# The first product of a gated mixing kernel: seven block products with shared sums, four of them split a second time, accumulated onto blocks in PSUM

## The chip, the cores and the metric

The kernel runs on one core of one Trainium2 chip. The metric is the device time of one execution in microseconds (us); lower is better. The core has TensorE (PE in the profile, with PEld for its weight loads), VectorE (DVE), ScalarE (ACT), GpSimd (POOL) and SyncE (SP), which issues most of the transfers (DMA). Operands lie in SBUF; a matmul adds its result into PSUM, which is as large as eight blocks of 128 x 512 float32, and DVE or ACT reads it from there.

## What is computed

```
a = x @ Cd.T ; b = x @ Sd.T          # x: 2048 x 1024, Cd, Sd: 1024 x 1024 (cosines, sines)
y = Cs @ a - Ss @ b                  # Cs, Ss: 2048 x 2048
h = relu(x @ w1 + b1) ** 2           # w1: 1024 x 3584
o = h @ w2 + b2                      # w2: 3584 x 1024
g = sigmoid((x * gate_w).sum(-1))
out = g * y + (1 - g) * o            # 2048 x 1024, all float32
```

The change touches the first line above all: x times the 1024 x 2048 matrix W that holds Cd and Sd side by side.

## The kernel before, in words

**Precision.** Every float32 operand is split in two halves of a faster matmul type: ScalarE copies it into `hi` (line 176), VectorE forms `lo` = operand - hi (line 194), and three matmuls (hi hi, hi lo, lo hi; line 261) take the place of one. Each operand that PE uses so costs one ACT copy and one DVE subtraction of 128 x 1024 elements.

**Blocks, steps and groups.** All data moves in blocks of 128 x 2 x 512 float32, of 512 KB. A *step* is the product of one stationary block with one moving block: 4 rows x 2 halves x 3 matmuls = 24 matmuls of 128 x 128 x 512. A `Group` is the set of steps that add up in the same two PSUM tiles (two banks each). When a group has run its `k` steps, its `done` function takes the two PSUM tiles up, the first after half of the last step (when two of the four rows are through), the second at its end. A tile taken up for the first time goes to SBUF as an ACT copy (line 285), later ones as a DVE addition or subtraction (line 287). A group may have several `done` functions: the PSUM tiles are then not cleared, and the next product adds to what they hold.

**Seven products for eight.** Each of the four matrix products is cut in 2 x 2 parts, and seven products of sums of parts replace eight products (tables `LEFT`, `RIGHT`, `INTO`; `INTO` says to which parts of the result a product is added). In `a1` (lines 304 to 360) the order is 2, 7, 4, 5, 6, 1, 3. Each of these products is itself 2 x 2 x 2 blocks: eight steps in four groups of two steps. Products 7 and 6 (`TWICE`) are cut a second time, and take seven steps in groups of one. That makes 5 x 8 + 2 x 7 = 54 steps in `a1`; the whole kernel has 362.

**Sums.** An `Operand` with two parts loads both and adds them on DVE (line 175); where the operation is an addition and the product is not the first, the second part is added by a GpSimd-issued accumulating DMA instead (line 157). For the products cut twice, class `Sum` makes the first-level sums (line 234) and `Operand` the second-level ones (line 175, `sum<-part`).

**Where blocks live.** SBUF has 55 slots (line 18); `take` and `give` (lines 85 to 93) hand them out first in, first out. The results `a` are stored to DRAM and loaded again in `a2`; the results `b` stay in SBUF. PSUM is a pool of four tiles of two banks, used in turn (lines 71 and 253): one group holds two.

**The order of the work.** Lines 537 to 608 write the program out, step by step. Before step i, blocks for steps up to i + 12 are loaded as far as slots are free; operands of step i + 3 are summed and copied to `hi` at the latest, `lo` of step i + 2 at the latest; earlier (up to nine steps) only while slots and the planner's own clock for DVE allow (lines 585 to 600). Then the step's matmuls and take-ups are written. The framework orders each engine's queue once more by when its model expects an instruction to be ready; the trace shows the order that came out. After `a1` follow `a2` (lines 400 to 441), and twice `h_stage` and `o_stage`.

Of the kernel before, what the change touches and what calls it, by code (L numbers as in the profile page):

```python
# [19 lines left out]
TWICE = (7, 6)  # L20
# [16 lines left out]


LEFT_A = {**LEFT, 1: ((0, 0), (1, 1), SUB), 6: ((1, 0), (0, 0), ADD), 7: ((0, 1), (1, 1), ADD)}
RIGHT_A = RIGHT  # L40
INTO_A = {1: ((0, 0, 1), (1, 1, -1)), 2: ((1, 0, 1), (1, 1, -1)), 3: ((0, 1, 1), (1, 1, -1)),
          4: ((0, 0, -1), (1, 0, 1)), 5: ((0, 0, -1), (0, 1, 1)), 6: ((1, 1, 1),), 7: ((0, 0, 1),)}
# [13 lines left out]
def gated_mix_kernel(ctx: ExitStack, tc: tile.TileContext, x4, xn, w4, ct, w1a, w1b, w2, b1, b2, gw, out):  # L56
# [14 lines left out]
    psum = ctx.enter_context(tc.tile_pool(name="psum", bufs=4, space=bass.MemoryType.PSUM))  # L71
    dram = ctx.enter_context(tc.tile_pool(name="dram", bufs=1, space=bass.MemoryType.DRAM))

    free = deque(ctx.enter_context(tc.tile_pool(name=f"slot{i}", bufs=1)) for i in range(SLOTS))
    home = {}
# [24 lines left out]
    class Near:  # L100


        def __init__(self, name):
            self.name, self.slot, self.uses, self.done = name, None, 0, False
# [20 lines left out]
    class Operand:  # L125


        def __init__(self, blocks, width=512, dma=False):
            self.width = width
            self.op = blocks[2] if len(blocks) == 3 else None  # L130
            self.blocks = list(blocks[:2]) if self.op else list(blocks[:1])
            self.added = None
            if dma and self.op == ADD:
                self.op, self.added = None, self.blocks.pop()
            self.uses = 0
            self.cuts = [(slice(0, 2), slice(0, width))]
            for b in self.blocks:
                if isinstance(b, Near):
                    b.uses += 1
# [14 lines left out]
        def load(self, engines):  # L154
            run(self.load_parts(engines))
            if self.added is not None:
                nc.gpsimd.dma_start(self.slots[0], self.added, accum_op=ADD)

        def extra(self):

            return max(2 + (self.op is not None) - self.room(), 0)

        def vector_time(self):
            return VEC[0] + VEC[1] * self.width / 512

        def sum_parts(self):
# [4 lines left out]
            self.src = src[0] if not self.op else mine[0] if mine else take("sum")  # L171
            self.hi = take("hi", F32R)
            for k, c in self.cuts:
                if self.op:
                    nc.vector.tensor_tensor(self.src[:, k, c], src[0][:, k, c], src[1][:, k, c], op=self.op)  # L175
                nc.scalar.activation(self.hi[:, k, c], self.src[:, k, c], AF.Copy)  # L176
                yield
            if self.op:
                give(*mine[1:])
                self.let_go()  # L180

        def sum(self):
            run(self.sum_parts())
            return self.vector_time() if self.op else 0.0

        def let_go(self):
            for b in self.blocks:
                if isinstance(b, Near):
                    b.used()

        def rest_parts(self):
            self.lo = take("lo", F32R)
            for k, c in self.cuts:
                nc.vector.tensor_tensor(self.lo[:, k, c], self.src[:, k, c], self.hi[:, k, c].bitcast(F32),  # L194
                                        op=SUB)
                yield
            if not self.op:
                self.let_go()
            if self.op or not isinstance(self.blocks[0], Near):
                give(self.src)  # L200

        def rest(self):
            run(self.rest_parts())
            return self.vector_time()
# [6 lines left out]
    class Sum(Near):  # L211


        def __init__(self, blocks):
            super().__init__("part")
            self.op = blocks[2] if len(blocks) == 3 else None
            self.blocks = list(blocks[:2]) if self.op else list(blocks[:1])

        def extra(self):
            return 0  # L220

        def room(self):
            return len(self.blocks)

        def load(self, engines):
            self.raws = [take("part") for b in self.blocks]
            for b, t in zip(self.blocks, self.raws):
                next(engines).dma_start(t, b)

        def sum(self):  # L230
            self.slot, self.done = self.raws[0], True
            if not self.op:
                return 0.0
            nc.vector.tensor_tensor(flat(self.slot), flat(self.slot), flat(self.raws[1]), op=self.op)
            give(self.raws[1])
            return VEC[0] + VEC[1]

        def rest(self):
            return 0.0

    class Group:


        def __init__(self, rows, k, *done):

            self.rows, self.k, self.done, self.at = rows, k, done, 0
# [3 lines left out]

        def run(self, st, mv, by_part=False):
            if self.at == 0:
                self.ps = [psum.tile([P, 2, 512], F32, name="ps") for _ in range(self.rows // 2)]
# [5 lines left out]
            for r, kk, n in mms:  # L259
                a, b = ((st.hi, mv.hi), (st.hi, mv.lo), (st.lo, mv.hi))[n]  # L260
                nc.tensor.matmul(self.ps[r // 2][:, r % 2, :], a[:, kk, r * P:(r + 1) * P],  # L261
                                 b[:, kk, :], start=self.at == 1 and kk + n == 0,
                                 stop=ends and kk == 1 and n == 2, skip_group_check=self.at > self.k)
                if ends and r % 2 and kk == 1 and n == 2:
                    self.done[self.at // self.k - 1][0](r // 2, self.ps[r // 2])

# [36 lines left out]

    def a1():
        order = (2, 7, 4, 5, 6, 1, 3)
        first, last = touches(order, INTO_A)
        def take_up(i, n, q, c, ps, sign, fresh, ends):
            near = ab[n, q, c]
            add_to(near.new() if fresh else near.slot, ps, -sign if n else sign, fresh)
            if ends:  # L310
                near.done = True
                if n == 0:
                    stores.append((a_far[q, c], near))

        def twice(p):

            order2 = (4, 3, 7, 1, 5, 6, 2)
            first2, last2 = touches(order2, CHAINED)
            part_a = {(m, q): Sum(blocks_of(LEFT_A[p], lambda i, j, m=m, q=q: x4[2 * i + m, j, q]))
                      for m in range(2) for q in range(2)}  # L320
            part_b = {(q, c): Sum(blocks_of(RIGHT_A[p], lambda j, n, c=c, q=q: w4[n, c, j, q]))
                      for c in range(2) for q in range(2)}
            groups = {}
            for p2 in order2:
                def done(p2):
                    def f(rp, ps):
                        for m, c, sign2 in CHAINED[p2]:
                            for i, n, sign in INTO_A[p]:
                                take_up(i, n, 4 * i + 2 * m + rp, c, ps, sign * sign2,
                                        first[i, n] == p and first2[m, c] == p2,  # L330
                                        last[i, n] == p and last2[m, c] == p2)
                    return f, 2 * sum(first[i, n] == p and first2[m, c] == p2
                                      for m, c, _ in CHAINED[p2] for i, n, _ in INTO_A[p])

                on = {4: 7, 1: 6}.get(p2)
                if p2 not in (7, 6):
                    groups[on] = group = Group(4, 1, *(done(e) for e in (p2, on) if e))
                else:
                    group = groups[p2]
                st = Operand(blocks_of(LEFT[p2], lambda m, q: part_a[m, q]))  # L340
                mv = Operand(blocks_of(RIGHT[p2], lambda q, c: part_b[q, c]))
                step(st, mv, group)

        for p in order:
            if p in TWICE:
                twice(p)
                continue
            mvs = [[Operand(blocks_of(RIGHT_A[p], lambda j, n, c=c, q=q: w4[n, c, j, q]), dma=p != order[0]) for q in range(2)]
                   for c in range(2)]
            for m in range(2):  # L350
                sts = [Operand(blocks_of(LEFT_A[p], lambda i, j, m=m, q=q: x4[2 * i + m, j, q]), dma=p != order[0])
                       for q in range(2)]
                for c in (m, 1 - m):
                    def done(rp, ps, p=p, m=m, c=c):
                        for i, n, sign in INTO_A[p]:
# [288 lines left out]
```

## Time and profile before

| what | value |
|---|---|
| median of 3 runs | 1988.97 us (1987.73 to 1989.03) |
| the profiled execution | 1988.42 us, of which the span is 1986.6 us |
| TensorE busy | 1972.6 us, 99% of the span, 8688 matmuls |
| VectorE busy | 1441.5 us, 73% |
| ScalarE busy | 824.2 us, 41% |
| moved by DMA | 421.97 MB, 212 GB/s |
| `a1` in the span | 0 to 306.3 us (1296 matmuls) |

The span is what the profile sees of the program; 1.8 us of the profiled execution lie around it. A row of the profile gives an instruction's own duration. Instructions of one engine overlap: five DVE additions in a row of 1.22 us each take 5.74 us, so one every 1.13 us, and matmuls of 390 ns follow one another every 227 ns.

### The profile page before, as it was taken

To read this page: it belongs to the slowest core of one execution; us is meant where nothing else is said; L and a number is where in the kernel's file an instruction comes from. 1 tells how busy PE (TensorE), PEld (TensorE's weight loads), DVE (VectorE), ACT (ScalarE), POOL (GpSimd) and SP (SyncE) were. 2 spreads that over 40 slices of the span, in tenths; PEclk is the share of its full clock that TensorE was granted. 3 is DMA by queue.
4 is the path that set the end of the run, shared out by engine and by line. 5 is a ranking of instruction groups with operands and counts; after the bars stand their busy time and mean duration, and the time that the engine had idled before them with its cause. 6 is when DMAs were issued, how large, how long until landed. Compare 5 with 4: busy or idle time off the path is not lost.

```text
span 1986.6 us, 22336 instructions
## 1 busy us (share of the span) xinstructions
PE 1972.6 (99%) x8688; PEld 1632.9 (82%) x8688; DVE 1441.5 (73%) x1331; ACT 824.2 (41%) x882; POOL 39.6 (2%) x72
## 2 busy tenths in 40 slices
PE   8999999999999999999999999999999999999999
PEld 6888888888888888888888888888888888888887
DVE  6988989467853579755565867789965667778795
ACT  5613222423432334334654563334456435633342
POOL 0010000000000000000000000000000000000000
PEclk9999999999999999999999999999999999999999
DMA  8673987367654469864454743558854566525671
GB/s 328 202 254 108 334 280 257 133 228 259 233 204 136 159 235 368 332 251 159 146 188 155 274 171 136 169 203 293 322 180 146 171 229 225 191 99 199 216 281 43
DMA packets 126570, 421.97 MB, mean 212 GB/s; under 512 B 13696, under 2 KB 26496, under 8 KB 126464
## 3 DMA queue, kind: packets, MB, share of 16 engines
q1 hardware_dynamic: 117600, 390.92, 55.5%
q0 software_dynamic: 8000, 28.32, 4.2%
q8 instruction: 68, 1.11, 0.2%
q10 hardware_dynamic: 864, 1.31, 0.2%
q14 instruction: 38, 0.31, 0.0%
HBM read 395.33 MB, written 25.17 MB: 212 GB/s over the span
## 4 chain that ended last, share of the span: by engine, by line
PE 99%; DMA 0%; DVE 0%; ACTq 0%; issue 0%; DVEq 0%
PE ps L261 99%; DMA raw<-in_x 0%; ACTq L151 0%; DVE lo L194 0%; DVE o L503 0%; DVEq L640 0%; DVE raw L175 0%; DVEq L194 0%
## 5 line engine op out<-in xcount | busy, mean ns | idle before, releaser
L261 PE MATMUL ps<-hi 128*128 128x512 f32 x2896 | 1127.9, 390 | 6.0 <-ACT hi L176 6.0
L261 PE MATMUL ps<-lo,hi 128*128 128x512 f32 x2896 | 1127.8, 390 | 3.4 <-DVE lo L194 3.4
L261 PE MATMUL ps<-hi,lo 128*128 128x512 f32 x2896 | 1127.7, 390 | 0.0
L176 ACT ACTIVATE hi<-raw 128x1024 fp32r<-128x1024 f32 (+2 forms) x433 | 435.3, 1024 | 797.5 <-PE ps L261 305.0
L261 PEld LDWEIGHTS ps<-hi 128*128 128x128 f32 x2896 | 544.4, 188 | 118.9 <-ACT hi L176 6.0
L261 PEld LDWEIGHTS ps<-lo,hi 128*128 128x128 f32 x2896 | 544.2, 188 | 116.9 <-DVE lo L194 4.2
L261 PEld LDWEIGHTS ps<-hi,lo 128*128 128x128 f32 x2896 | 544.3, 188 | 112.9
L194 DVE TENSOR_TENSOR lo<-raw,hi 128x1024 fp32r<-128x1024 f32 (+2 forms) x433 | 502.2, 1181 | 168.8 <-PE ps L261 69.3
L175 DVE TENSOR_TENSOR raw<-raw 128x1024 f32<-128x1024 f32 (+2 forms) x276 | 322.9, 1177 | 189.8 <-DMA raw<-in_ct 57.9
L287 DVE TENSOR_TENSOR h<-h,ps 128x1024 f32<-128x1024 f32 x84 | 102.3, 1218 | 78.3 <-ACT h L285 45.3
L176 ACT ACTIVATE hi<-sum 128x1024 fp32r<-128x1024 f32 x98 | 103.7, 1060 | 118.3 <-DVE sum L175 99.5
L194 DVE TENSOR_TENSOR lo<-sum,hi 128x1024 fp32r<-128x1024 f32 x98 | 119.6, 1223 | 15.8 <-ACT hi L176 10.2
L463 ACT ACTIVATE h<-h,b1c 128x512 f32<-128x512 f32 x112 | 74.7, 714 | 66.7 <-DVE h L287 66.5
L175 DVE TENSOR_TENSOR sum<-h 128x1024 f32<-128x1024 f32 x70 | 85.4, 1222 | 0.4
L285 ACT ACTIVATE h<-ps 128x1024 f32<-128x1024 f32 x56 | 55.4, 1022 | 48.6 <-PE ps L261 48.6
L465 ACT ACTIVATE h<-h 128x1024 f32<-128x1024 f32 x56 | 58.9, 1052 | 0.8
L503 DVE SCALAR_TENSOR_TENSOR o<-ps,omg,o 128x512 f32<-128x512 f32 x64 | 44.5, 746 | 18.8 <-PE ps L261 18.8
L287 DVE TENSOR_TENSOR a<-a,ps 128x1024 f32<-128x1024 f32 x44 | 52.3, 1217 | 5.2 <-PE ps L261 5.2
L287 DVE TENSOR_TENSOR b<-b,ps 128x1024 f32<-128x1024 f32 x44 | 51.9, 1218 | 0.0
L194 DVE TENSOR_TENSOR lo<-h,hi 128x1024 fp32r<-128x1024 f32 x28 | 34.2, 1221 | 7.5 <-PE ps L261 5.8
L583 POOL DMA_DIRECT2D out<-o x28 | 15.1, 541 | 1014.5 <-DVE o L503 1012.8
L176 ACT ACTIVATE hi<-h 128x1024 fp32r<-128x1024 f32 x28 | 29.3, 1048 | 12.8 <-PE ps L261 12.8
(31 smaller groups left out, 299.9 us busy)
## 6 DMA issues: line engine op xcount, KB each, us to landing
raw<-in_w SPq DMA_DIRECT2D x195, 512.0 KB, 4.5
raw<-in_ct SPq DMA_DIRECT2D x192, 512.0 KB, 5.0
raw<-in_w1a SPq DMA_DIRECT2D x144, 512.0 KB, 4.7
raw<-in_x SPq DMA_DIRECT2D x74, 512.0 KB, 4.7
raw<-a SPq DMA_DIRECT2D x48, 512.0 KB, 4.6
raw<-in_w1b SPq DMA_DIRECT2D x48, 256.0 KB, 3.5
part<-in_w SPq DMA_DIRECT2D x16, 512.0 KB, 9.3
part<-in_x SPq DMA_DIRECT2D x16, 512.0 KB, 8.7
```

The costliest lines, as they stand in the source:

```text
L175: nc.vector.tensor_tensor(self.src[:, k, c], src[0][:, k, c], src[1][:, k, c], op=self.op)
L176: nc.scalar.activation(self.hi[:, k, c], self.src[:, k, c], AF.Copy)
L194: nc.vector.tensor_tensor(self.lo[:, k, c], self.src[:, k, c], self.hi[:, k, c].bitcast(F32), op=SUB)
L261: nc.tensor.matmul(self.ps[r // 2][:, r % 2, :], a[:, kk, r * P:(r + 1) * P], b[:, kk, :], start=self.at == 1 and kk + n == 0, stop=ends a ...
L285: nc.scalar.activation(flat(dst), flat(ps), AF.Copy, scale=float(sign))
L287: nc.vector.tensor_tensor(flat(dst), flat(dst), flat(ps), op=ADD if sign > 0 else SUB)
L463: nc.scalar.activation(dst[:, rr, :], dst[:, rr, :], AF.Relu, bias=b1c[:, f_:f_ + 1])
L465: nc.scalar.activation(flat(dst), flat(dst), AF.Square)
L503: nc.vector.scalar_tensor_tensor(dst[:, rr, :], ps[:, rr, :], (omg if sign > 0 else nomg)[:, t:t + 1], dst[:, rr, :], op0=ALU.mult, op1=AL ...
L583: nc.gpsimd.dma_start(dst, src)
```

## The change

It changes only how `a1` is computed, and what that needs in the helpers.

- *Sums built on one another.* The seven products of `a1` get new factors (`FACTORS`): S1 = A21 + A22, S2 = S1 - A11, S3 = A11 - A21, S4 = A12 - S2, and T1 to T4 alike; they are kept in slots and used again (classes `Sums` and `Part`). Products 1 and 2 take plain parts. No sum is made by an accumulating DMA any more.
- *Four products cut twice.* 1, 5, 3 and 4 run as seven steps each, 2, 6 and 7 as eight: 4 x 7 + 3 x 8 = 52 steps, in the order 1, 2, 5, 3, 6, 7, 4. The second level uses the same tables.
- *Additions in PSUM.* Within a product cut twice, steps 1, 6, 7, 4 share one group (`chain`) and add up in its two tiles; 5 and 3 share another (`other`); 2 has its own (`last`). The order of its steps is 5, 1, 3, 6, 2, 7, 4; for the very first product 1, 5, 3, 6, 2, 7, 4.
- *Products that add to copied blocks.* A group may start `onto` blocks: ACT copies them from SBUF into PSUM (`Group.prepare`, one step ahead), and the matmuls add to them. Products 2, 6 and 7 start onto the eight blocks `part` that hold product 1 (later the sums with it), and step `last` of products 1 and 5.
- *Helpers.* `Operand` is cut in `Part` (load and sum) and `Operand` (`hi` and `lo`); the list of the planner so has up to two entries for an operand of every stage. PSUM tiles come from a list `banks` instead of a rotating pool. Signs in `a2` are moved from the take-up of `b` to `LEFT_C` and `CHAINED_C`; the number of its operations stays.

```diff
-TWICE = (7, 6)
+SUMS_L = {"S1": ((1, 0), (1, 1), ADD), "S2": ("S1", (0, 0), SUB), "S3": ((0, 0), (1, 0), SUB),
+          "S4": ((0, 1), "S2", SUB)}
+SUMS_R = {"T1": ((0, 1), (0, 0), SUB), "T2": ((1, 1), "T1", SUB), "T3": ((1, 1), (0, 1), SUB),
+          "T4": ((1, 0), "T2", SUB)}
+FACTORS = {1: ((0, 0), (0, 0)), 2: ((0, 1), (1, 0)), 3: ("S4", (1, 1)), 4: ((1, 1), "T4"), 5: ("S1", "T1"),
+           6: ("S2", "T2"), 7: ("S3", "T3")}
...
+        def prepare(self):
+            if self.ps is None and len(banks) >= self.rows // 2 and all(b.begun for b in self.onto or ()):
+                pools = [banks.popleft() for _ in range(self.rows // 2)]
+                self.ps = [b.tile([P, 2, 512], F32, name="ps", tag="ps") for b in pools]
+                self.pools = pools
+                for b, t in zip(self.onto or (), self.ps):
+                    nc.scalar.activation(flat(t), flat(b.slot), AF.Copy)
...
-                                 b[:, kk, :], start=self.at == 1 and kk + n == 0,
+                                 b[:, kk, :], start=self.at == 1 and kk + n == 0 and not self.onto,
...
+        def put(dst, ps, ends=False, sign=1):
+            add_to(dst.slot or dst.new(), ps, sign, True)
+            finish(dst, ends)
+
+        def add(dst, ps, ends=False, src=None, sign=1):
+            if src is None:
+                add_to(dst.slot, ps, sign, False)
+            else:
+                nc.vector.tensor_tensor(flat(dst.slot or dst.new()), flat(src.slot), flat(ps), op=ADD)
+                vec(1.22)
+            finish(dst, ends)
...
+        def twice(p, old, new, ends, drop=False):
+            l, r = FACTORS[p]
+            l2 = Sums(lambda m, q: left[m, q].of(l), SUMS_L, True)
+            r2 = Sums(lambda q, c: right[q, c].of(r), SUMS_R, True)
+
+            def takes(first, *where, ends=False):
+                def f(rp, ps):
+                    for m, c in where:
+                        if not first:
+                            add(new[m, c, rp], ps, ends)
+                        elif old:
+                            add(new[m, c, rp], ps, ends, old[m, c, rp])
+                            if drop:
+                                old[m, c, rp].drop()
+                        else:
+                            put(new[m, c, rp], ps, ends)
+                return f, 2 * first * len(where)
+
+            chain = Group(4, 1, takes(True, (0, 0)), takes(False, (0, 1), ends=ends), takes(False, (1, 1), ends=ends),
+                          takes(True, (1, 0), ends=ends))
+            other = Group(4, 1, takes(True, (1, 1)), takes(True, (0, 1)))
+            if old:
+                last = Group(4, 1, takes(False, (0, 0), ends=ends))
+            else:
+                last = Group(4, 1, (lambda rp, ps: put(new[0, 0, rp], ps, ends), 0),
+                             onto=[new[0, 0, rp] for rp in range(2)])
+            begin = ((5, other), (1, chain))
+            for p2, group in (*(begin if steps else begin[::-1]), (3, other), (6, chain), (2, last), (7, chain),
+                              (4, chain)):
+                l_, r_ = FACTORS[p2]
+                step(l2.operand(l_), r2.operand(r_), group)
+
+        def six(k, ps):
+            put(part[k], ps)
+            add(c12[k], ps, True)
+
+        def seven(k, ps):
+            put(part[k], ps)
+            add(c22[k], ps, True)
+
+        twice(1, None, part, False)
+        direct(2, part, 2, lambda k, ps: put(c11[k], ps, True))
+        twice(5, None, c22, False)
+        twice(3, c22, c12, False)
+        direct(6, part, 0, six)
+        direct(7, part, 0, seven)
+        twice(4, part, c21, True, True)
...
+        if 0 <= i < n - 1:
+            steps[i + 1][2].prepare()
```

`direct` runs a product as eight steps in four groups of two, onto the blocks given; `c11` to `c22` are the four parts of the result, of which `c11` and `c21` (the `a`) are stored to DRAM.

More of the change, by code (lines that the diff above doesn't have):

```diff
@@ L302, in gated_mix_kernel @@
     a_far = {(q, c): Kept(f"a{q}{c}") for q in range(8) for c in range(2)}
-    def a1():
[L305 to L309, printed above, removed]
-            if ends:
[L311 to L349, printed above, removed]
@@ L350, in a1 @@
             for m in range(2):
[L351 to L352 removed]
+                sts = [left[m, q].operand(l) for q in range(2)]
                 for c in (m, 1 - m):
[L354 to L358 removed]
+                    group = Group(4, 2, (lambda rp, ps, m=m, c=c: take_up((m, c, rp), ps), slots),
+                                  onto=onto and [onto[m, c, rp] for rp in range(2)])
@@ L401, in a2 @@
         order = (2, 4, 7, 5, 3, 1, 6)
-        first, last = touches(order, CHAINED)
+        first, last = touches(order, CHAINED_C)
         y = {k: Near("y") for k in gy}
@@ L593, in gated_mix_kernel @@
                     break
-                if any(isinstance(b, Near) and not b.done for b in getattr(o, "blocks", ())):
+                if not lo and not ready(o):
                     break
```

220 lines of the change are left out of this document (124 added, 96 removed).

## The prediction, made before the change was run

> **What bounds the kernel now.** First the page's busy shares and its chain of waits, then the chain in order of time, then the waits of PE alone.
>
> ```profile
> PE 1972.6 (99%) x8688; PEld 1632.9 (82%) x8688; DVE 1441.5 (73%) x1331; ACT 824.2 (41%) x882; POOL 39.6 (2%) x72
> ```
> ```profile
> 9.54 1.03 DVE lo L194 x2
> 10.57 0.04 issue
> 10.62 1971.39 PE ps L261 x8686
> 1982.01 0.03 issue
> ```
> ```profile
> PE ps L261 <- ACT hi L176: 6.0, 1, 6.0
> PE ps L261 <- DVE lo L194: 3.4, 1, 3.4
> ```
>
> From 10.62 us on PE runs without a gap; its only two waits lie before. So time is the number of matmuls, the start, and 4.6 us behind the last matmul. Any stall that the change brings is added in full, and no cheaper DVE, ACT or DMA work shortens anything behind the start. The start, by PE's timeline:
>
> ```profile
> 5.96 1.22 PE L261 MATMUL ps<-hi 128*128 128x512 f32 x2 [5.96 <-ACT hi L176]
> 10.62 1.22 PE L261 MATMUL ps<-lo,hi 128*128 128x512 f32 x2 [3.44 <-DVE lo L194]
> ...
> 14.20 1.05 PE L261 MATMUL ps<-hi,lo 128*128 128x512 f32 x2
> 15.05 1.27 PE L261 MATMUL ps<-hi 128*128 128x512 f32 x4
> 16.16 1.08 PE L261 MATMUL ps<-lo,hi 128*128 128x512 f32 x4
> ```
>
> Between 10.62 and 15.05 a matmul starts every 0.43 us, later every 0.23. The windows count 33 matmuls up to 20.0; the other 8655 end at 1982.0, so 0.2267 us each and 5.44 us a step; step k (from 0) ends at 12.52 + 5.44 (k + 1). The slow 10 cost 10 x 0.2 = 2 us.
>
> How tight DVE is, by windows of the products of `a1` (the sixth is the product 6, cut twice) and DVE's timeline in that product:
>
> ```profile
> 137.70:181.20 43.50, 43.50 (x193) 36.03 (x192) 34.14 (x30) 17.36 (x17) 1.06 (x2) 1.00 0.27 97
> 181.20:219.30 38.10, 38.10 (x170) 31.56 (x169) 36.36 (x32) 10.48 (x11) 3.51 (x4) 1.00 0.94 296
> ```
> ```profile
> 213.72 1.22 DVE L175 TENSOR_TENSOR raw<-raw 128x1024 f32<-128x1024 f32 x1
> 214.86 2.35 DVE L287 TENSOR_TENSOR b<-b,ps 128x1024 f32<-128x1024 f32 x2
> ```
>
> Third and fifth figures are the window and DVE: 36.4 of 38.1 us. Product 6 needs 52 DVE operations (8 sums of the first level, 10 of the second, 14 `lo`, 20 take-ups), at one per 1.14 us (five in a row take 5.74) 59 us. DVE managed because it was busy for 34 of 43.5 us in the window before, whose own product 5 has 16 operations (18 us): some 14 were done ahead. Its take-ups came late: step 36 is half through at 211.1, and its first addition starts at 214.86, 3.7 us later. Nobody waited, since between two products in one PSUM group another step always ran.
>
> **The change part by part.**
>
> *Steps.* Of 54 steps in `a1` 52 stay (4 x 7 + 3 x 8): 48 matmuls less, 48 x 0.2267 = 10.9 us off PE, which sets the end. Certain, if PE stays fed.
>
> *Start.* Before, the first step needs two x blocks, their sum and a w block (1.5 MB), and DVE's `lo` waited behind the additions at 7.04 and 8.94. Afterwards it needs one x and one w block and no sum. The w half landed at 5.28, its `hi` took 0.63; so PE could run from about 7 instead of 10.6, 3.6 us earlier at best. The second step then needs three blocks and two sums (T1, S1): at DVE's 13.15 the before had six blocks landed, the after needs five by then; at 0.41 MB per us (the DMA rate after 8 us) that is 1.2 us earlier, about 12; then sum 1.22, `hi` 1.06, `lo` 1.22 makes 15.5, where step 1 began at 17.96. Step 1 and 2 share the group `other`, so step 2 also waits for ACT to read half-way results of step 1: 1.03 us, inside the half step of 2.7 us if ACT's queue is free. The best is -3.6, and +2 if ACT copies of a few later operands go first; I take -2.5, the second step's gain.
>
> *DVE in `a1`.* Before: 52 sums, 68 `lo`, 88 take-ups = 208, as the groups by line count them. Afterwards: first level 8 sums for each of four blocks = 32, second level 8 in each of four products = 32, `lo` 4 x 14 + 3 x 8 = 80, take-ups 4 + 4 + 14 + 14 + 8 + 8 = 52: 196, so 12 x 1.14 = 14 us less in a stage 11 us shorter: 79% against 81%. Off the path in the mean. But by product: 1: 26; 2: 8; 5: 34; 3: 44; 6: 20; 7: 24; 4: 40, where seven steps hold 33 and eight hold 38. So 5, 3 and 4 are over what fits by 1, 11 and 7 operations (1, 12, 8 us) and live on work done ahead in 2, 6 and 7, as product 6 does now.
>
> *Back to back.* New is that steps 7 and 4 of a product cut twice follow each other in the group `chain`: PE may not write a tile before DVE has added it up (1.22 us). The first tile is ready after half a step, so DVE may be 2.72 - 1.22 - 0.1 = 1.4 us late; any more PE waits. No such wait is in the trace. Queued behind it on PE is everything; on DVE ahead of it what belongs to the next three steps. Bounds, from DVE's lateness in the trace: 0 (0.7 us late at 184.65) to 3.7 - 1.4 = 2.3 us each; if DVE does nothing before the planner's latest time, more. In product 4 it then has five operations in most steps, where 4.8 fit, and once six: at the sixth step it is 2.3 us behind, has four operations (4.5 us) ahead of the addition, and ends that 1.25 + 2.3 + 4.5 + 1.15 = 9.2 us after step 5, 3.8 after step 6. The same count gives 3 us in product 3, and 5 in product 5, where 12 operations stand between two take-ups. In products 1 and 5 the step before is taken up by ACT, which leaves DVE free to run ahead. I take 0, 0, 2 and 2 us for products 1, 5, 3 and 4, the lateness that the trace shows: 4 us.
>
> The Trainium skill (TensorE: Matmul & The Clock Gate, section "What's actually happening") speaks against waits of this length: the array runs at half pace until some 3.4 us of work have passed, and again after an idle window as long. The rows of the start agree (3.44 us idle, then 4.4 us slow); a PE that has run at full pace and goes slow again is in no row. By the rule, waits of 2 us cost no more than themselves and the sum stays; one of 3.8 or 5 us would cost 2 us more, 1981 instead of 1979 for one such, and 1991 instead of 1987 in rival A.
>
> *ACT.* `hi` 68 to 80, take-ups 32 to 44, and 28 copies into PSUM: 100 to 152, 54 us more, on an engine that is busy 112 of 306 us; no ACT row writes PSUM, the nearest are 1.03 (PSUM to SBUF) and 1.06 (SBUF to SBUF), so 1.0 each. They run a step ahead of use; cover 5.4 us against 2.1 for two. Zero, up to 1 us at each of 14 pairs if ACT's queue is held up; I take 0.
>
> *DMA.* Loads 96 to 72, and eight accumulating ones on POOL's queue gone: nothing waits for them on PE, so 0. *Behind `a1`* counts are the same; `lo` is planned one operand closer to its `hi`. PE had two steps (10.9 us) of cover; 0, up to +4 in the stages where DVE is over 90%.
>
> *Sum* against the profiled execution: 1988.42 - 10.9 - 2.5 + 4 = **1979.0** (span 1977.2). That execution is 0.55 below the median of 1988.97, which I leave inside the error.
>
> **Rivals.**
>
> *A. PE waits at every back-to-back pair.* For: 3.7 us late in a lighter place. Against: sums can run ahead. 5 + 3 + 3.8 = 11.8; 1988.4 - 10.9 - 2.5 + 11.8 = 1987; no change.
>
> *B. DVE becomes the bound in products 5, 3 and 4, slower than before.* Place: 55 slots. Through product 3 kept blocks are 8 `part`, 8 `c22`, up to 8 `c12`, S2, S4, T1 and a plain part 4 each: 40, where product 6 of before has 24 results and 8 parts. With `hi` and `lo` of four steps (14) nothing is left to work ahead with, and loads wait for slots that PE has just left. Price: 34 + 44 = 78 operations, 88.9 us in 76.2, and 40, 45.6 in 38.1: +20.2 if none is ahead; with -10.9 and a start at 0: 1997.7. It decides from 9 operations ahead downwards (10.9 / 1.14 = 9.6 fewer than needed). Against: before, some 14 were carried into product 6, with 24 results and 8 parts kept.
>
> *C. The start is lost.* If ACT's queue keeps the program's order, the copy that frees `other` stands behind `hi` of the next three steps, which wait for DVE's sums: nine DVE operations (1.2) and ten ACT ones (1.0) in a row from the first sum at 9.3, so step 2 at 30.1 instead of 23.4, +6.7, and 2 for the slow matmuls after such a gap: 1988.4 - 10.9 + 8.7 + 4 = 1990; no change. Against: in the trace a `hi` (22.75) runs between the take-ups of two tiles (21.84, 23.69), which the program writes later, so queues are filled by readiness.
>
> **How the numbers follow.** Forecast 0.52, A 0.2, B 0.18, C 0.1. A difference under 0.2% (4 us) can't be told from no change. A is split, as its waits may be a little shorter: 0.06 of it ends below 1985. Faster 0.52 + 0.06 = 0.58, same 0.14 + 0.1 = 0.24, slower 0.18. The range goes from the best start without a wait, 1988.4 - 10.9 - 3.6 = 1973.9, to part-way into B (half of its 20 us and no gain at the start: 1987.6, all of it 1997.7): 1973 to 1995. The forecast's own is 1973 to 1984.
>
> **What would show it.** 8640 matmuls; PE's first long run from about 7; waits of PE for DVE's take-ups ahead of the last step of products 3 and 4, some 4 us in sum. Waits of PE on `lo` in products 5, 3, 4 speak for B; a gap of over 5 us before 35 us for C. Wrong at all: PE waits behind 300 us.

## The result, and the profile after

| | before | after |
|---|---|---|
| median | 1988.60 us (1987.73 to 1989.03, 4 runs) | 1975.42 us (1974.86 to 1975.97, 4 runs) |
| profiled execution | 1988.42 us, span 1986.6 | 1975.97 us, span 1974.1 |
| matmuls | 8688 | 8640 |
| DVE operations | 1331 | 1317 |
| ACT operations | 882 | 934 |

The ratio is 0.9934, with a 95% interval of 0.9917 to 0.9951: the change makes the kernel 13.2 us faster by the medians, 12.5 by the two profiled executions. The forecast of 1979.0 is 3.6 us above the median.

The busy shares of the changed kernel first; the line answers to the first one shown of before.

```profile
PE 1962.6 (99%) x8640; PEld 1623.7 (82%) x8640; DVE 1427.4 (72%) x1317; ACT 874.5 (44%) x934; POOL 32.5 (2%) x64
```

Then its chain in order of time (start, length, what).

```profile
20.94 1.02 ACT u L292
21.96 0.04 issue
22.00 1947.37 PE ps L265 x8590
1969.38 0.03 issue
```

And the waits of PE (total us, number of times, longest).

```profile
PE ps L265 <- ACT hi L207: 6.4, 3, 5.8
PE ps L265 <- DVE lo L217: 0.2, 1, 0.2
PE ps L265 <- ACT u L292: 0.2, 1, 0.2
```

The reader is to see that the picture of before has stayed: from 22.00 us to the end PE runs 8590 of its 8640 matmuls without a gap, at 1947.37 / 8590 = 0.2267 us each, the pace of before to the last digit. All the waits lie ahead of 22 us, or end there, and but for the first (5.8 us, up to the first operands) they are four and add to 0.96 us. What the change could cost on DVE, ACT and DMA has cost nothing behind that point.

So the difference has two parts. **Steps:** 48 matmuls x 0.2267 = 10.9 us. **Start:** 50 matmuls are through when the 51st starts at 22.00. In before 33 were through at 20.0, so its 51st started at 20.0 + 17 x 0.2267 = 23.85: 1.85 us. Together 12.7; the stretch behind the last matmul is 0.1 us longer, and the spans differ by 12.5. The start by PE's timeline:

```profile
5.81 1.22 PE L265 MATMUL ps<-hi 128*128 128x512 f32 x2 [5.81 <-ACT hi L207]
...
11.09 1.39 PE L265 MATMUL ps<-hi 128*128 128x512 f32 x4
...
14.54 0.50 PE L265 MATMUL ps<-hi 128*128 128x512 f32 x1 [0.24 <-ACT hi L207]
...
15.93 0.50 PE L265 MATMUL ps<-hi,lo 128*128 128x512 f32 x1 [0.20 <-DVE lo L217]
...
21.09 0.73 PE L265 MATMUL ps<-hi 128*128 128x512 f32 x2 [0.34 <-ACT hi L207]
22.00 0.50 PE L265 MATMUL ps<-hi 128*128 128x512 f32 x1 [0.18 <-ACT u L292]
```

PE's first run starts at 5.81, where before had to wait until 10.62 for the `lo` of a sum. Its first twelve matmuls, at some 0.44 us each, are through at 11.09; the first twelve of before at 15.05. Of these 4 us a good half is lost again up to 22, mostly at the four waits: they fall on matmuls 25 and 29, in the second step, and 49 and 51, at the beginning of the third. Matmuls overlap, so such a wait costs more than its idle time: from the start of one matmul to that of the next the four take 0.57 to 0.72 us, where the pace is 0.23, which makes 1.6 us. The start differs a little between executions: the same first 50 matmuls are through at 21.4 in the profiles of `late1` and `late3` below, at 22.0 in this one, which is of the slowest of the four runs. By the medians the start is worth 13.2 - 10.9 = 2.3 us.

The windows by product that answer to the two shown of before: products 2, 5, 3 and 4 (window; its length and PE; PEld; DVE; ACT; POOL; clock; DMA share; GB/s).

```profile
48.80:92.30 43.50, 43.50 (x194) 36.03 (x193) 29.29 (x26) 23.63 (x24) 3.87 (x7) 1.00 0.43 156
92.30:130.40 38.10, 38.10 (x170) 31.56 (x169) 29.26 (x25) 23.65 (x24) 0.53 (x1) 1.00 0.24 85
130.40:168.40 38.00, 38.00 (x170) 31.46 (x169) 36.82 (x33) 15.34 (x15) 0.00 (x0) 1.00 0.45 152
...
255.50:293.60 38.10, 38.10 (x170) 31.56 (x169) 37.74 (x35) 11.82 (x12) 3.19 (x6) 1.00 0.73 254
```

The prediction counted what each product needs of DVE: 8 operations in product 2, then 34, 44 and, for product 4, 40. The windows show what DVE did: 26, 25, 33 and 35. It did 18 operations ahead in product 2 and lived on them in 5 and 3. With all seven windows (34, 26, 25, 33, 30, 23, 35 done; 26, 8, 34, 44, 20, 24, 40 needed) DVE is some 8, 26, 17, 6, 16, 15 and 10 operations ahead at the end of each product; the least is 6, behind product 3. (The windows begin at 10.7 us, and an operation that crosses a border counts in both, so these are good to a few.) PE is busy for the whole of every window but product 1's (37.1 of 38.1 us, the start), DVE for 97% and 99% in products 3 and 4. (Of the two windows of before that the prediction shows, the second is that of product 6, the fifth product in order.)

### The profile page after: what moved, and what is told of

Its sections match the earlier page's. It is cut to its first block, busy times and chain, and to the rows that moved or that the text cites. A ratio compares the mean times of both kernels' runs of the same rounds, so it can differ in the third digit from the quotient of the medians.

```text
span 1974.1 us, 22174 instructions
## 1 busy us (share of the span) xinstructions
PE 1962.6 (99%) x8640; PEld 1623.7 (82%) x8640; DVE 1427.4 (72%) x1317; ACT 874.5 (44%) x934; POOL 32.5 (2%) x64
## 4 chain that ended last, share of the span: by engine, by line
PE 99%; DMA 1%; ACT 0%; DVE 0%; DVEq 0%; issue 0%
PE ps L265 99%; DMA raw<-in_w 0%; ACT hi L207 0%; DMA raw<-in_x 0%; ACT u L292 0%; DVE o L569 0%; DVEq L720 0%
## 5 line engine op out<-in xcount | busy, mean ns | idle before, releaser
L207 ACT ACTIVATE hi<-raw 128x1024 fp32r<-128x1024 f32 (+2 forms) x441 | 443.3, 1023 | 683.4 <-DVE raw L172 263.7
L217 DVE TENSOR_TENSOR lo<-raw,hi 128x1024 fp32r<-128x1024 f32 (+2 forms) x441 | 511.1, 1179 | 159.9 <-PE ps L265 93.3
L172 DVE TENSOR_TENSOR raw<-raw 128x1024 f32<-128x1024 f32 x290 | 341.2, 1183 | 194.0 <-DMA raw<-in_ct 74.1
L207 ACT ACTIVATE hi<-sum 128x1024 fp32r<-128x1024 f32 x110 | 115.9, 1058 | 165.3 <-PE ps L265 81.6
L217 DVE TENSOR_TENSOR lo<-sum,hi 128x1024 fp32r<-128x1024 f32 x110 | 133.7, 1219 | 19.6 <-PE ps L265 9.3
L294 DVE TENSOR_TENSOR b<-b,ps 128x1024 f32<-128x1024 f32 x26 | 31.6, 1216 | 10.7 <-ACT u L292 8.8
L292 ACT ACTIVATE u<-ps 128x1024 f32<-128x1024 f32 x26 | 26.4, 1019 | 26.1 <-PE ps L265 26.1
L294 DVE TENSOR_TENSOR y<-y,ps 128x1024 f32<-128x1024 f32 x24 | 28.7, 1215 | 6.8 <-PE ps L265 6.8
```

Source lines behind the costliest of these rows:

```text
L172: nc.vector.tensor_tensor(self.slot[:, k, c], src[0][:, k, c], src[1][:, k, c], op=self.op)
L207: nc.scalar.activation(self.hi[:, k, c], self.block.slot[:, k, c], AF.Copy)
L217: nc.vector.tensor_tensor(self.lo[:, k, c], self.block.slot[:, k, c], self.hi[:, k, c].bitcast(F32), op=SUB)
L292: nc.scalar.activation(flat(dst), flat(ps), AF.Copy, scale=float(sign))
L294: nc.vector.tensor_tensor(flat(dst), flat(dst), flat(ps), op=ADD if sign > 0 else SUB)
```

## The experiments

The kernel before was run beside every group of these; its medians there are 1988.58 to 1988.69, so that medians of different groups may be compared. The theory put to the test: *the gain is the number of matmuls and the start, and nothing is lost because DVE's work of the heavy products is done ahead.* The rivals: the gain comes from the copies into PSUM, which unburden DVE; or there are waits at the back-to-back steps, and something else pays for them.

**Fewer products cut twice, in the old scheme.** `none_twice` is the kernel before with

```diff
-TWICE = (7, 6)
+TWICE = ()
```

> The kernel before with no product of the first stage cut twice: 56 steps there instead of 54. Theory 1 (PE runs without a gap, so time is the number of matmuls): 48 matmuls of 0.2267 us more, +10.9 us over before, about 1999.5, PE again unbroken from some 10 us on. Theory 2 (part of the gain came from work taken off DVE, ACT or the transfers): less than +10.9, since DVE loses the second-level sums, 12 lo and many take-ups.

Measured 2001.77 us (ratio 1.0069, 1.0046 to 1.0092), 13.1 over before. 10.9 are the 48 matmuls more; the other 2.2 are, up to 0.1, one wait that PE has here and not there, by its timeline:

```profile
156.35 0.47 PE L261 MATMUL ps<-hi 128*128 128x512 f32 x1 [1.93 <-DVE a L287]
```

So two steps are worth 10.9 us, both ways. The size of the steps' term is confirmed, and the extra wait shows that waits add in full.

**More of them, in the old scheme.** `old_four_twice` makes the same 8640 matmuls as the change, with the sums and take-ups of before:

```diff
-TWICE = (7, 6)
+TWICE = (7, 4, 5, 6)
```

> The kernel before with four products cut twice (7, 4, 5, 6) and nothing else of the change: 52 steps, as many matmuls as after the change. If the number of steps alone decides, 1988.6 - 10.9 = 1977.7. Theory 1 with DVE's limit: products 4 and 5 then need 68 and 60 DVE operations where seven steps hold 33; 292 in all, 333 us in a stage of 283 us, so PE waits for DVE by some 40 to 50 us: about 2020.

Measured 2056.46 us (ratio 1.034, 1.031 to 1.037): slower than before by 68 us, and than the change by 81, with the same number of matmuls. The windows of it, in the columns as above:

```profile
150.00:200.00 50.00, 34.24 (x121) 25.91 (x120) 50.00 (x46) 20.58 (x21) 2.13 (x4) 0.83 0.49 175
200.00:250.00 50.00, 32.69 (x106) 24.99 (x105) 50.00 (x45) 8.25 (x8) 0.00 (x0) 0.76 0.19 67
```

DVE is busy in every moment and PE for two thirds. My number was too small since it spread the surplus over all of `a1`: DVE is ahead of PE again only when 36 of the 52 steps are through, and the light products that come last can't take over work of those before them. The other part is the clock, below: behind 25 us PE's gaps make 56 us, and matmuls at half pace 22. What makes four products cut twice pay is thus not the cutting, it is that the new sums and take-ups cost DVE so little. (The order of the products differs too, and no run separates it; but in no order do 292 operations of 1.14 us, 333 us, fit into a stage of 283.)

**Are the copies into PSUM what saves DVE?** `no_psum_start` starts no product on copied blocks. DVE adds instead: 28 operations more on DVE, 56 fewer on ACT.

```diff
+        def onto_sum(dst, k, ps):
+            add(part[k], ps)
+            nc.vector.tensor_tensor(flat(dst[k].slot), flat(dst[k].slot), flat(part[k].slot), op=ADD)
...
         def six(k, ps):
-            put(part[k], ps)
-            add(c12[k], ps, True)
+            onto_sum(c12, k, ps)
...
-        direct(6, part, 0, six)
...
+        direct(6, None, 0, six)
...
```

(Products 7 and 2 and the group `last` likewise.)

> The changed kernel without products that start on copied blocks: no copy into PSUM, DVE adds instead (28 operations more: 224 in the first stage, 255 of 283 us; ACT loses 56). Theory 1 (DVE is near its limit in products 5, 3 and 4 and late by 1.1 to 1.7 us at the steps that follow each other in one PSUM group): PE waits some 1 to 6 us in sum, 1976.5 to 1981.5. Rival (the copies were not needed, DVE has room): 1975.4.

Measured 1974.96 us (ratio 0.993, 0.9908 to 0.9953). A miss: no time is lost, and PE runs unbroken from 21.28. DVE has 224 operations in `a1` then, more than in before, and carries them: 24 of the 28 fall into products 2, 6 and 7, in which it had time left. Its window of product 2, with 37 operations where the change had 26:

```profile
48.80:92.30 43.50, 43.50 (x193) 36.03 (x193) 40.79 (x37) 12.89 (x13) 3.87 (x7) 1.00 0.38 146
```

So the copies into PSUM are not what the gain comes from; with 8640 matmuls and shared sums it is there without them. The rival falls.

**One product more, or fewer slots.** `five_twice` cuts product 2 a second time too: 51 steps, 24 matmuls less.

```diff
-        direct(2, part, 2, lambda k, ps: put(c11[k], ps, True))
+        twice(2, part, c11, True)
```

> The changed kernel with product 2 cut twice too: 51 steps. If PE stays fed: 1975.4 - 5.4 = 1970. Theory 1 (DVE is the next bound): products 1, 2, 5 and 3 need 26 + 36 + 34 + 44 = 140 DVE operations, 160 us, in 28 steps of 152 us, and product 2 no longer leaves DVE time to work ahead: PE waits 7 to 14 us, 1977 to 1984.

Measured 1978.01 us (ratio 0.9949, 0.9926 to 0.9972): 2.6 us slower than the change with 5.4 us less for PE to do. Two windows of it:

```profile
48.80:87.00 38.20, 36.70 (x162) 30.05 (x161) 37.97 (x34) 10.39 (x10) 3.34 (x6) 1.00 0.59 199
87.00:125.00 38.00, 35.19 (x156) 28.82 (x154) 37.81 (x35) 23.59 (x24) 1.06 (x2) 1.00 0.39 147
```

Where the change had its light product, in which DVE worked ahead, DVE is now full and PE is not; PE runs unbroken only from 165.94. This is the mechanism of rival B, one product further than where the prediction feared it.

`slots50` leaves the change as it is, with fewer blocks in SBUF:

```diff
-    SLOTS, KEEP = 55, 5
+    SLOTS, KEEP = 50, 5
```

> The changed kernel with 50 slots instead of 55. If DVE lives on work done ahead and slots limit it: lateness grows by some operations and PE waits 1 to 6 us, 1976.5 to 1981.5, most of it in products 3 and 4. If slots don't limit it: 1975.4.

Measured 1979.07 us (1977.56 to 1981.17; ratio 0.995, 0.993 to 0.9969), 3.7 over the change. That lies in the range expected if slots limit how far DVE can be ahead, but it doesn't show this: PE stops at the end of `a1`, when the operands of `a2` are loaded late, and not in products 3 and 4; DVE had stood idle for 5.0 us, up to 297.57. PE's timeline there (profiled execution: 1981.17, the slowest of the four; the others lie 2.1 to 4.5 over the change, and have no profile):

```profile
298.73 0.39 PE L265 MATMUL ps<-hi,lo 128*128 128x512 f32 x1
301.67 0.47 PE L265 MATMUL ps<-hi 128*128 128x512 f32 x1 [2.55 <-ACT hi L207]
...
302.90 0.41 PE L265 MATMUL ps<-hi,lo 128*128 128x512 f32 x1
303.13 0.61 PE L265 MATMUL ps<-hi 128*128 128x512 f32 x1
303.54 0.63 PE L265 MATMUL ps<-lo,hi 128*128 128x512 f32 x1
```

A gap of 2.55 us, and 1.5 us behind it the matmuls fall to the pace of 0.43 us for 3.4 us: 8 x 0.2 = 1.6 more. Together 4.2 of the 5.2 us by which this execution is longer.

**Is DVE late at the back-to-back steps?** In the change, the half of step 5 that ends product 1's tile is through at 40.6 (step k ends at 10.67 + 5.44 (k + 1), half a step less for the first tile); the same half of steps 20, 27 and 50 at 122.2, 160.3 and 285.4. DVE's timeline has the additions that PE must await, of products 1, 5, 3 and 4, at

```profile
40.92 1.22 DVE L294 TENSOR_TENSOR u<-u,ps 128x1024 f32<-128x1024 f32 x1
...
123.34 1.21 DVE L294 TENSOR_TENSOR b<-b,ps 128x1024 f32<-128x1024 f32 x1
...
161.36 1.21 DVE L294 TENSOR_TENSOR b<-b,ps 128x1024 f32<-128x1024 f32 x1
...
287.10 2.56 DVE L294 TENSOR_TENSOR a<-a,ps 128x1024 f32<-128x1024 f32 x2
```

so 0.3, 1.1, 1.1 and 1.7 us late, where the prediction gave a margin of 1.4. Are these lucky, or near an edge? `late1` and `late3` put one and three DVE operations more into the first take-up of each of the four pairs (the addition in 2 or 4 parts of weight 1/2 or 1/4; the sum is the same):

```diff
+                        if not first and (m, c, rp) == (1, 1, 0):
+                            t = flat(new[m, c, rp].slot)
+                            for _ in range(4):
+                                nc.vector.scalar_tensor_tensor(t, flat(ps), 0.25, t, op0=ALU.mult, op1=ALU.add)
...
```

(this is `late3`; `late1` has 2 and 0.5.)

> The changed kernel with one more DVE operation (1.14 us) ahead of the end of the take-up that the last step of each product cut twice waits for (the first tile of step 7, taken up in two halves of weight 0.5). Theory 1 (DVE is late there by 0.3, 1.1, 1.1 and 1.7 us in products 1, 5, 3 and 4, and PE has 1.4 us to spare): waits of 0, 0.8, 0.8 and 1.4, so +3.0: 1978.4. Rival (DVE recovers, the margin is wider than the rows say): 1975.4.

> The same with three more DVE operations at each of the four places (3.4 us). Theory 1: waits of 2.3, 3.1, 3.1 and 3.7, so +12.2: 1987.6. By the Trainium skill (TensorE: Matmul & The Clock Gate) a wait over some 3.4 us would be followed by slow matmuls. Rival (DVE recovers): under +6.

Measured 1975.69 us (ratio 0.9934, 0.9911 to 0.9956) and 1975.79 (0.9935, 0.9912 to 0.9957). Both are misses: no loss, and no wait of PE at any of the four places (`late1` has one of 0.45 us at 737 us, far behind `a1`). Something hid them. In the built program the order of PE's queue is not that of the code. At the end of product 1, with the number of matmuls on each of the two tiles of a group:

```
the change:    chain 12 + 12 | chain 12 + 12 | next 12 + 12
late3:         chain 12 + 12 | next 11 | chain, second tile 12 | next 4 | chain, first tile 12 | next 9
```

The framework, which expects the late addition, has put 15 matmuls of product 2 and the second tile ahead of the tile that is taken up late: 27 x 0.2267 = 6.1 us of cover. (In `late1` it put 6 ahead there.) `pinned` and `pinned_late3` take that freedom away, the first from the change, the second from `late3`: PE's queue keeps the order of the code from the fourth step to the first of `a2`.

```diff
-                nc.tensor.matmul(self.ps[r // 2][:, r % 2, :], a[:, kk, r * P:(r + 1) * P],
+                mm = nc.tensor.matmul(self.ps[r // 2][:, r % 2, :], a[:, kk, r * P:(r + 1) * P],
...
+                if pin:
+                    tc.keep_in_program_order(mm)
...
```

> The changed kernel with the matmuls of the first stage (from its fourth step on) kept on PE's queue in the order in which the code writes them. In the changed kernel the queue holds some matmuls of the following step ahead of a step that would wait (2 of them ahead of the last step of product 4). Theory 1 (that reordering, and a small margin, hide DVE's lateness): PE now waits 0.3 to 3 us in sum ahead of the last steps of products 5, 3 and 4: 1975.7 to 1978.4. Rival (DVE is in time in any order): 1975.4.

> The same order, with the three more DVE operations of late3 at each of the four places. Theory 1 (in late3 PE filled the time with matmuls of the next step that the queue put ahead, 34 pieces of a queue cut up where before it was 9): now PE waits 2.3, 3.1, 3.1 and 3.7 us: 1975.4 + 12.2 = 1987.6, up to 1 us more for slow matmuls after the gaps. Rival (DVE catches up by itself): 1975.8 as late3.

Measured 1975.79 us (ratio 0.9935, 0.9918 to 0.9953) and 2009.93 (1.0105, 1.0089 to 1.0121). The same window at the end of product 1, first of `late3`, then of `pinned_late3`:

```profile
40.00:50.00 10.00, 10.00 (x46) 8.29 (x45) 10.00 (x10) 3.19 (x4) 0.00 (x0) 1.00 0.34 138
```
```profile
40.00:50.00 10.00, 3.92 (x15) 2.91 (x15) 10.00 (x10) 1.98 (x3) 0.00 (x0) 0.88 0.34 135
```

DVE does ten operations in both; PE does 46 matmuls in the one and 15 in the other. PE's gap in `pinned_late3`, and DVE in it:

```profile
42.54 0.39 PE L265 MATMUL ps<-hi,lo 128*128 128x512 f32 x1
49.02 0.77 PE L265 MATMUL ps<-hi 128*128 128x512 f32 x1 [6.08 <-ACT hi L207]
```
```profile
40.86 1.22 DVE L392 SCALAR_TENSOR_TENSOR u<-ps,u 128x1024 f32<-128x1024 f32 x1
41.99 1.21 DVE L172 TENSOR_TENSOR raw<-raw 128x1024 f32<-128x1024 f32 x1
43.12 1.22 DVE L392 SCALAR_TENSOR_TENSOR u<-ps,u 128x1024 f32<-128x1024 f32 x1
44.26 1.21 DVE L296 TENSOR_TENSOR u<-u,ps 128x1024 f32<-128x1024 f32 x1
45.39 1.22 DVE L392 SCALAR_TENSOR_TENSOR u<-ps,u 128x1024 f32<-128x1024 f32 x1
46.52 1.22 DVE L172 TENSOR_TENSOR raw<-raw 128x1024 f32<-128x1024 f32 x1
47.65 1.22 DVE L392 SCALAR_TENSOR_TENSOR u<-ps,u 128x1024 f32<-128x1024 f32 x1
```

The wait is put down to ACT's `hi`, which had long been done; what ended it is the fourth part, at 48.87. My number for `pinned_late3` was too small by a factor of three: I counted the four parts alone, but DVE's queue has other operations between them. Four such gaps, from the start of one matmul to that of the next and less the pace (6.2, 5.4, 6.4 and 7.2 us), make 25.2 us, and the slow matmuls behind them, 39 of them at half pace, 9.7. Together 34.9; it was 0.6 ahead of the change at the 51st matmul, and the spans differ by 34.0.

`pinned` has one wait of 1.3 us, up to 21.0, where the change has its four small ones. At three of the four places PE doesn't wait. At the fourth, the end of product 4, the first matmul of the last step starts 0.45 us after the one before it, where the pace is 0.23; DVE's addition for it starts at 286.56, as late by the same count as in the change:

```profile
287.47 0.39 PE L265 MATMUL ps<-hi,lo 128*128 128x512 f32 x1
287.92 0.47 PE L265 MATMUL ps<-hi 128*128 128x512 f32 x1
```

That is a loss of 0.2 us, as 1.7 us of lateness and a margin of 1.4 would have it. So both hold: in products 1, 5 and 3 DVE is late by less than the margin, and where it exceeds the margin, by 0.3 us in product 4, two matmuls that PE's queue puts ahead cover it.

**Three attempts at more.** `plain_first` runs the first product's second level with the plain products 1 and 2 first (1, 2, 5, 6, 3, 7, 4), so that sums are needed later:

```diff
...
+            if not steps:
+                last = Group(4, 1, takes(False, (0, 0)))
+                chain.done = (takes(True, (0, 0)), takes(True, (0, 1)), *chain.done[2:])
+                other.done = (other.done[0], takes(False, (0, 1)))
+                order = ((1, chain), (2, last), (5, other), (6, chain), (3, other), (7, chain), (4, chain))
...
```

> The changed kernel with another order in the first product: steps 1, 2, 5, 6, 3, 7, 4, so that the first two steps need plain blocks only and no two steps of the group other follow each other. Theory 1 (the start is bound by transfers, ACT and DVE, and PE waited 0.96 us in it): the waits go, -0.5 to -1.0: 1974.4 to 1974.9. Rival (transfers of four blocks come no sooner): 1975.4.

Measured 1975.25 us (ratio 0.9932, 0.9909 to 0.9954): the unbroken run starts at 21.78, released by a row of `lo` on DVE, with matmul 53, which the change starts at 22.58. But the profiles of `late3` and `late1`, with the change's own start, have it at 21.97 and 22.01, and the medians differ by 0.2 us, within the spread: no gain is shown, a miss. `warm_plain_first` adds 36 matmuls of a zero 128 x 128 tile into an unused PSUM tile ahead of the first real one, to have PE warm at 5.8.

```diff
+    for _ in range(36):
+        nc.tensor.matmul(wps[:, 0, :128], colder, colder, start=True, stop=True)
```

> plain_first with 36 matmuls of zeros of 128 x 128 on PE before the first operand has landed (from about 1.5 us on). Theory 1 (the 10 slow matmuls at the start are a cold clock, and with two plain steps first the operands keep up): the run from 5.8 us on is at 0.23 us a matmul, the first step ends 2 us sooner; the second step's blocks land at about 10 to 12 us, so 0.5 to 2 us are gained: 1973.3 to 1974.8. Rival (transfers bound the start): 1975.3.

Measured 1976.2 us (ratio 0.9937, 0.9919 to 0.9955); a miss. PE's timeline:

```profile
1.25 7.94 PE L97 MATMUL ps<-colder 128*128 128x128 f32 x36 [1.25 <-DVE colder L94]
8.99 1.16 PE L273 MATMUL ps<-hi 128*128 128x512 f32 x2
...
11.66 0.68 PE L273 MATMUL ps<-hi 128*128 128x512 f32 x2
```

The 36 take 0.22 us each, so they keep the first real matmul back from 5.7 to 8.99, and 7.7 us of them do not warm PE: the real ones still run at half pace until 11.66. (The granted clock reads 1.00 there, as it does in the slow start of before; at the start only the pace tells.) Whether it is their size, their zeros or their spacing stays open, and so does what a working warm-up would bring.

`five_twice_pool` gives 32 sums of the first level in `five_twice` to GpSimd, to take the surplus off DVE:

```diff
-                    nc.vector.tensor_tensor(self.slot[:, k, c], src[0][:, k, c], src[1][:, k, c], op=self.op)
+                    (nc.gpsimd if self.far else nc.vector).tensor_tensor(
+                        self.slot[:, k, c], src[0][:, k, c], src[1][:, k, c], op=self.op)
...
```

> Five products cut twice as in five_twice, with the 32 first-level sums moved from DVE to GpSimd (POOL), which is busy 2% of the span. DVE then has 192 operations in the first stage instead of 224. Theory 1 (five_twice lost its 5.4 us and 2.6 more to DVE's surplus in products 1, 2, 5 and 3): PE unbroken again, 1970 to 1971.5. Rival (an addition on POOL, of which no row shows the time, is several us long or holds DVE up): PE waits for sums, 1975 to 1985.

Measured 2006.24 us (ratio 1.0086, 1.007 to 1.0102), 28 us slower than `five_twice`; outside both numbers, though the slower one's mechanism is what is seen. Its groups up to 330 us (count, busy us, mean ns):

```profile
L173 POOL TENSOR_TENSOR raw<-raw 128x1024 f32<-128x1024 f32 x32 | 93.1, 2921 | 144.3 <-DMA raw<-in_w 84.6 <-DMA raw<-in_x 42.8 <-ACT hi L209 10.7
...
L219 DVE TENSOR_TENSOR lo<-raw,hi 128x1024 fp32r<-128x1024 f32 x49 | 71.4, 1473 | 8.9 <-ACT hi L209 5.2 <-PE ps L267 3.7
...
L296 DVE TENSOR_TENSOR b<-b,ps 128x1024 f32<-128x1024 f32 x26 | 31.4, 1213 | 23.4 <-ACT u L294 23.4
```

An addition takes 2.92 us on GpSimd, and DVE's own `lo`, with both inputs in SBUF, rise from 1.22 us in `five_twice` to 1.47 on average, while DVE's additions with one input in PSUM keep their 1.21. That fits the Trainium skill (GPSIMD Engine Reference, section "Key points"), by which GpSimd shares its SBUF interfaces with VectorE and contends with instructions that have two SBUF inputs. So DVE got 32 operations less and lost as much in the others: it is busy for 1459.7 us, against 1457.6 in `five_twice`. PE waits for the late sums and take-ups: behind 25 us its gaps make 24 us, and matmuls at half pace 9; no run parts what is due to the long additions from what is due to DVE's slower ones. No version here beats the change by more than its spread.

## Why the prediction was right, point by point

- **What bounds the kernel: right.** PE's unbroken run, its pace and the stretch behind it are the same; every experiment's loss is gaps of PE, matmuls more, and matmuls at half pace, and next to nothing else (`slots50` also ends 0.5 us later behind its last matmul).
- **Steps, -10.9: right** to a tenth, by the 8640 matmuls at 0.2267 us, and by `none_twice` in the other direction.
- **Start, -2.5: direction right, size -1.85 in the profiled execution, -2.3 by the medians.** PE could start even earlier (5.81, not about 7), and the second step began at 14.54, 3.5 us before that of the old kernel, not 2.5. But the prediction took the second step's gain as the last word, and the four small waits in it and at the third, for ACT's `hi` twice, for a `lo` and for a take-up, took 1.6 us back.
- **Back to back, +4: this step failed.** "I take 0, 0, 2 and 2 us for products 1, 5, 3 and 4, the lateness that the trace shows". Measured: 0 at all four, and 0.2 at one when PE's queue is held to the order of the code. The term was mis-sized: its lateness of 3.7 us came from a place of the old kernel where nobody waited for DVE, so nothing there had asked for an earlier addition. In the change DVE is 0.3 to 1.7 us late. The margin of 1.4 us was worked out rightly, as `pinned` shows, but for the queue: at the end of product 4 the addition that starts at 287.10 ends at 288.3, and PE would want the tile at 285.4 + 2.7 = 288.1, but two matmuls of `a2` stand ahead of the tile in PE's queue. The prediction knew that queues are filled by readiness, used it for ACT in rival C, and did not ask what it means for PE. `pinned_late3` shows the price that it set against this term to be real, and larger than thought, in a kernel where PE can't be given other work. Against the profiled execution the forecast is 3.0 us too long: these 4, less the 0.65 us by which it had taken the start's gain too large. Its range holds the time with or without such waits, so the number alone would not have told.
- **DVE in the heavy products.** The prediction counted 12 operations fewer; the page has 14 fewer over the whole kernel. What the counts by product were not held against is the work ahead: some 17 operations in hand where product 3 had 11 too many, some 15 where product 4 had 7. That is what kept rival B out, and the room is not large: one more product cut twice loses 2.6 us. (50 slots lose 3.7, but at the start of `a2`.)
- **ACT, 0; DMA, 0; behind `a1`, 0: right.** No wait of PE lies behind 22 us. The copies cost 1.03 us each on an engine that is busy for 157 of the first 295 us.
- **Rival A** is out by the four additions; **C** by the start: no gap of PE above 0.34 us behind 5.81.
- **The clock.** The prediction said that no row shows a PE that was at full pace and goes slow again. Now there are such rows, in `old_four_twice`:

```profile
162.67 0.39 PE L261 MATMUL ps<-hi,lo 128*128 128x512 f32 x1
169.50 0.76 PE L261 MATMUL ps<-hi 128*128 128x512 f32 x1 [6.45 <-DVE a L287]
170.07 0.63 PE L261 MATMUL ps<-lo,hi 128*128 128x512 f32 x1
```

After 6.45 us of idleness the matmuls come every 0.43 us, and the granted clock of the window 169.4 to 171.4 is 0.50. After the 1.93 us of `none_twice` they keep to 0.23. The rule of the Trainium skill that the prediction cited (TensorE: Matmul & The Clock Gate, section "What's actually happening") agrees with these two. With the gap of 2.55 us in `slots50`, shorter than its idle window of about 3.4, it does not: eight matmuls went slow there, at a granted clock of 0.51. Nor does it with two gaps of `five_twice_pool`, of 2.29 and 2.11 us; the first:

```profile
94.19 0.77 PE L267 MATMUL ps<-hi 128*128 128x512 f32 x1 [2.29 <-DVE a L296]
94.76 0.63 PE L267 MATMUL ps<-lo,hi 128*128 128x512 f32 x1
```

Seven matmuls or so behind each come at 0.43 us, at a granted clock of 0.50. But the gap of 2.87 us that ends at 125.07 in `five_twice` was followed by none, at a clock of 1.00. The measurement decides: gaps of 2.1 to 2.9 us cost some 1.6 us more than themselves in three cases here and nothing more in two (the other is one of 2.26 us in `five_twice_pool`), so in this range the length alone does not tell. The prediction's "waits of 2 us cost no more than themselves" is thus not safe; it did the forecast no harm, as no such wait came.

## What to carry to other kernels

Where one engine runs without a gap, price a change by the number of its instructions, and then ask only whether the others still deliver in time; for that compare, stage by stage, the operations that they must do with those that they have in hand, not the mean load. A wait for a buffer cost nothing here as long as the queue of the waiting engine could be given other work ahead of it, so look at the order of the built queue before pricing such a wait. A cut that saves matmuls pays only if its sums and take-ups are cheap enough for the engine that makes them: the same 8640 matmuls took 1975 us with one set of sums and one order of products, and 2056 with the other.

## What the runs showed of the hardware that was not expected

- ACT writes PSUM no faster than it reads it. The change's group of copies into PSUM, from the groups by line with the forms kept apart:

```profile
L254 ACT ACTIVATE ps<-u 128x1024 f32<-128x1024 f32 x26 | 26.5, 1026 | 8.6 <-DVE b L294 8.1 <-DVE b L356 0.2
```

  1.026 us, where PSUM to SBUF takes 1.02 and SBUF to SBUF 1.06.
- Gaps of 2.11, 2.29 and 2.55 us were enough to bring a warm PE back to half pace, while one of 2.87 was not. The slow matmuls began at once behind the gap of 2.29 us, but 0.6 us after PE had resumed behind that of 2.11, and 1.5 us after behind that of 2.55.
- 36 matmuls of a zero 128 x 128 tile over 7.9 us did not bring PE to full pace.
- Beside GpSimd's additions of 2.92 us, DVE's `lo`, with two SBUF inputs, took a fifth longer (1.47 us against 1.22), and its additions with a PSUM input (1.21) no longer.
